# Norms of a fifth chunk off TensorE, Gram sums of batch 0 in other PSUM banks, and a new schedule, in a fused attention and gated-feed-forward kernel

## The chip, the cores and the metric

The kernel runs on one core of one Trainium2 chip. The metric is the device time of one execution in microseconds (us). The kernel before takes 273.9 us (median of three runs, 273.01 to 275.34). Every ratio below comes from runs of both kernels taken in the same rounds on the same chip.

The engines are named as the profile names them: PE is TensorE (PEld its weight loads), DVE is VectorE, ACT is ScalarE, POOL is GpSimd and SP is SyncE. A "q" behind a name means that engine's instruction queue, for instance SPq for a DMA that SyncE issues.

## The reference, cut to what matters

```python
B, N, C = 4, 6336, 256                      # q, k, v: f32
qn = q / (norm(q, axis=1) + 1e-6)           # norms over the N rows
kn = k / (norm(k, axis=1) + 1e-6)
a  = softmax(kn.T @ qn / tau)               # 256 x 256 for each batch
x  = v @ a                                  # B*N rows of 256
H  = maximum(x @ w_h, 0)
T  = sigmoid(x @ w_t + b_t)
out = T * H + (1 - T) * x                   # f32
```

All the attention is over channels, so each batch has two stages. Stage 1 sums k^T q, k^T k and q^T q over 6336 rows. Stage 2 multiplies the rows of v by three 256 x 256 matrices (a, a @ w_h, a @ w_t) and puts the results together. A pair is two blocks of 128 rows, and a chunk is 4 pairs (1024 rows); a batch has 6 chunks and a short rest. Chunks are counted through all batches, from 0 to 23.

## The kernel before

A small planner in the kernel's source puts some thousands of tasks in an order for each engine. Every task has a priority, the buffers that it takes and the buffers that it gives back. The parts that the argument touches follow, with cuts marked.

The numbers that the planner works with:

```python
O_BUFS = 7        # output buffers, 1 MB each, one chunk of 4 pairs of rows
LAG = 5           # a chunk's store is held until this many chunks later have begun
UNTIL = 65        # from this slot (pair number) on, stores are no longer held
AHEAD = 15        # a DMA transpose of v is issued so many slots ahead
BY_DMA = 1        # last batch: chunks of v from this one on are transposed by DMA
APART = 4         # chunks of a batch whose q norms are made off TensorE
V_AHEAD = -2
PRIO = {"tr": (-3.47, -0.36), "ev": (3.23, 2.26), ...}   # cut
```

Stage 1. Each step is 128 rows of q and k; the third matmul gives the q norms, and it is left out for chunks below `APART`, whose squares ACT and POOL make:

```python
def stage1(b, s):
    if s == order_of(b)[0]:
        sg_t[b] = [new(f"sg{c}", [P, 512], f32, f"sg{c}_{b}") for c in range(2)]
    ...
    for c in range(2):
        nc.tensor.matmul(sg[c][:, 0:C], kc, qa, start=first, stop=False)
        nc.tensor.matmul(sg[c][:, C : C + P], kc, kc, start=False, stop=False)
        if not apart(b, s // CH):
            nc.tensor.matmul(sg[c][:, C + P : C + 2 * P], qa[:, cs], qa[:, cs], ...)

def apart(b, j):
    return b > 0 and j < APART
```

The output. `result` is DVE's last instruction for a pair of rows, and the first of a chunk takes a fresh output buffer. SyncE stores the chunk and, when the store has landed, the buffer is free:

```python
def new(tag, shape, dt, name):
    return pool_of.get(tag, work).tile(shape, dt, tag=tag, bufs=nbuf[tag], name=name)

def result(b, i):
    ...
    if o == 0:
        og[(b, j)] = new("o", [P, CH, C], f32, f"o{b}_{j}")
    nc.vector.scalar_tensor_tensor(out=ot, in0=h, scalar=0.0, in1=pp, op0=max, op1=subtract)  # cut
```

So that stores do not take the DMA engines from the loads too early, they are held. A copy of 1 KB out of chunk n sits in SyncE's queue ahead of the store of chunk n - LAG. It cannot be issued before DVE has written the first result of chunk n, and the store behind it waits with it:

```python
def hold(b, j):
    nc.sync.dma_start(out=held_row, in_=og[(b, j)][0:1, 0, :])

def plan_holds():
    for x, b, j in chunk_stores:
        n = b * NJ + j + LAG
        y, g = begun.get(n, (None, 1e9))
        if g > UNTIL:
            x.key = max(x.key, UNTIL + 1.6)
            continue
        x.key = g + 1.6
        plan.add("SP", g + 1.5, 0.1, 0, [y], lambda n=n: hold(n // NJ, n % NJ), size=1024)
```

Of the kernel before, what the change touches and what calls it, by code (L numbers as in the profile page):

```python
# [15 lines left out]
P = 128  # L16
# [3 lines left out]
O_BUFS = 7  # L20
LAG = 5
UNTIL = 65
AHEAD = 15
BY_DMA = 1
MOVE = 150e3
APART = 4
V_AHEAD = -2

PRIO = {
    "tr": (-3.47, -0.36), "ev": (3.23, 2.26), "h": (0.45, 0.69), "bias": (3.3, -0.05),  # L30
    "t": (-0.22, 4.42), "relu": (-3.45, 3.58), "x": (-1.14, 3.11), "gate": (2.73, -4.04),
    "prod": (1.3, -1.18), "res": (4.05, 6.98), "s1": (1.48, 0.05), "sq": (6.77, 9.48),
}
POW = 0.75
HEAD = 6
TAIL = 63
EV = BIAS = ("ACT", "DVE")
ENDS = [17.5, 46, 64.5]

# [13 lines left out]
class Task:  # L53
# [6 lines left out]
    def __init__(self, eng, key, pitch, lat, deps, fn, take=(), drop=(), size=0, follows=()):  # L60
        self.eng, self.key, self.pitch, self.lat = eng, key, pitch, lat
        self.deps, self.fn, self.take, self.drop, self.size = deps, fn, take, drop, size
        self.follows = follows
        self.start = self.done = None
        self.soft = False
        self.held = {}
        self.serial = False
# [11 lines left out]
class Plan:  # L79
# [23 lines left out]
    def run(self):  # L103
# [43 lines left out]
        def pick(e):  # L147
            quiet = e == "POOL" and held(self.sums_stop)
            best = min(
                (x for x in avail[e] if ready(x) and not (quiet and x.soft)),  # L150
                key=lambda x: (x.key, x.n), default=None,
            )
            lst = in_order.get(e)
            if best is None and lst and ready(lst[-1]) and not (e == "POOL" and held(self.loads_stop)):
                return lst[-1]
            return best

        def held(stops):
            return any(
                a.start is not None and (b.done is None or b.done > t + eps) for a, b in stops  # L160
            )

        while left or any(queues.values()):
# [38 lines left out]
            for qq in act:  # L202
                if qq[0][1] < 1.0:
                    x = qq.pop(0)[0]
                    finish(x, t + self.LAG)
                    if x.eng == "POOL":
                        lanes[x.lane] = t + self.LAG
# [5 lines left out]
def kernel(  # L213
# [142 lines left out]
    consts = plan.add("POOL", len(plan.tasks), 0.6, 1.5, [], constants)  # L356
    consts.serial = True
    for j in range(1, NJ - 1):
        plan_load("q", 0, j)
        plan_load("k", 0, j)  # L360
    for nm in "qk":
        plan_load(nm, 0, NJ)
    for part in range(4):
        plan_load("q", 0, NJ - 1, 4, part)
        plan_load("k", 0, NJ - 1, 4, part)
    plan_load("q", 1, 0)
    plan_load("k", 1, 0)
    w_ld = [
# [3 lines left out]
        for m, w in enumerate((moe_w_h, moe_w_t))  # L372
    ]
    b_ld = [
        plan.add("POOL", len(plan.tasks), 0.54, 0, [], lambda u=u: load_b(u), size=40000)
        for u in range(2)
    ]
# [35 lines left out]
    def order_of(b):  # L413
# [4 lines left out]
        return [*range(S - CH), *range(S, NS), *range(S - CH, S)]  # L418

    def stage1(b, s):  # L420



        if s == order_of(b)[0]:
            sg_t[b] = [new(f"sg{c}", [P, 512], f32, f"sg{c}_{b}") for c in range(2)]
        sg = sg_t[b]
# [14 lines left out]
    def apart(b, j):  # L441
        return b > 0 and j < APART

# [25 lines left out]
    def plan_squares(b):  # L469

        ends, x = {}, None
        for j in range(APART):
            key = slot_of((b - 1) * NS + CH * j) + PRIO["sq"][0]
            parts = [
                plan.add(
# [5 lines left out]
            ends[j] = parts  # L481
            n0 = len(plan.tasks)
            y = plan.add(
# [7 lines left out]
            for z in plan.tasks[n0:]:  # L491
                z.soft = True
        def over_partitions():
# [22 lines left out]

    def plan_chain(b, first, last, key, sums_of_q):

# [82 lines left out]

        gs = act(copy_g, 0.58, 0.7, [dk], drop=[(first, "sg0"), (first, "sg1")])
        iq = dve(lambda: (recip(0), dcat()), 0.82, 0.92, [nq, dk])
# [310 lines left out]
    def plan_stage1(b):  # L914
        x = first = None
        part_ends, sums_of_q = ({}, []) if not apart(b, 0) else plan_squares(b)
        for n, s in enumerate(order_of(b)):
            key = -100 + n if b == 0 else slot_of((b - 1) * NS + s) + PRIO["s1"][0]
            deps = loaded("q", b, s) + loaded("k", b, s) + ([x] if x else [])
            x = plan.add(  # L920
                "PE", key, 0.33 if apart(b, s // CH) else 0.44, 0.66, deps, lambda s=s: stage1(b, s),
                take=["sg0", "sg1"] if n == 0 else [],
                drop=([] if apart(b, s // CH) else drops("q", b, s)) + drops("k", b, s),
            )
            x.lat = x.pitch if n < NS - 1 else 0.66
            if apart(b, s // CH) and s % CH == CH - 1:
                plan.add("NONE", 0, 0, 0, [x] + part_ends[s // CH], None, drop=drops("q", b, s))
            first = first or x
        ready[b] = plan_chain(b, first, x, -50, [sums_of_q] if apart(b, 0) else [])
        if b == B - 1:  # L930
            ends_of["sg0"] = ends_of["sg1"] = [x]
# [140 lines left out]
```

## Time and profile before

| | before |
|---|---|
| time, median (runs) | 273.9 us (273.01 to 275.34) |
| span of the profiled run | 271.6 us, clock 0.985 |
| PE's work, by start-to-start times | 239.0 us |
| PE: first matmul, last matmul | 9.0 us, 263.8 us |
| from the last matmul to the end | 7.8 us |
| 1 MB store, issue to landing, median | 9.1 us |

"PE's work" is not the busy time of the page. It adds the distance from each matmul's start to the next where the two follow each other closely, and counts the rest as lost. First start + work + lost = last start: 9.0 + 239.0 + 15.9 = 263.8 us (rounded).

The prediction below shows the page and the stretch around 40 us. What it does not show, and what also belong here, are two rows of the page: DVE's last instruction of a pair (L858) among the costliest groups, with its idle time after the second bar, and the store among the DMA issues.

```profile
L858 DVE SCALAR_TENSOR_TENSOR o<-h,pp 128x512 f32<-128x512 f32 x96 | 65.3, 687 | 1.9
L435 PE MATMUL sg<-q 128*128 128x128 f16 x192 | 42.8, 223 | 0.0
...
out_dram<-o SPq DMA_DIRECT2D x23, 1024.0 KB, 9.1
```

DVE waited only 1.9 us in all ahead of 96 such instructions: output buffers were always free in time. And here is the same kernel by stretch of time (the columns are the stretch, its length, then busy us and instruction count of PE, PEld, DVE, ACT and POOL, the granted clock, the DMA share and the GB/s written):

```profile
110.00:140.00 30.00, 30.00 (x308) 27.58 (x306) 23.09 (x41) 26.58 (x47) 21.00 (x23) 1.00 1.06 267
140.00:170.00 30.00, 29.67 (x301) 26.40 (x299) 24.16 (x61) 25.19 (x48) 16.13 (x19) 1.00 1.06 263
...
200.00:230.00 30.00, 29.48 (x279) 25.32 (x278) 23.47 (x58) 25.27 (x54) 4.09 (x7) 1.00 1.05 306
```

In these stretches PE is full, or nearly so, at full clock.

SyncE's own timeline shows how a held store leaves. Columns are start, length, engine and line; L897 is the 1 KB copy that holds, L872 the store.

```profile
124.93 0.51 SPq L897 DMA_DIRECT2D held_row<-o  x1
125.48 0.58 SPq L872 DMA_DIRECT2D out_dram<-o  x1
```

Chunk 7's first result was written at 124.21 us; the store that it releases was issued 1.27 us later.

### The profile page before, as it was taken

To read this page: it belongs to the slowest core of one execution; us is meant where nothing else is said; L and a number is where in the kernel's file an instruction comes from. 1 tells how busy PE (TensorE), PEld (TensorE's weight loads), DVE (VectorE), ACT (ScalarE), POOL (GpSimd) and SP (SyncE) were. 2 spreads that over 40 slices of the span, in tenths; PEclk is the share of its full clock that TensorE was granted. 3 is DMA by queue.
4 is the path that set the end of the run, shared out by engine and by line. 5 is a ranking of instruction groups with operands and counts; after the bars stand their busy time and mean duration, and the time that the engine had idled before them with its cause. 6 is when DMAs were issued, how large, how long until landed. Compare 5 with 4: busy or idle time off the path is not lost.

```text
span 271.6 us, 6265 instructions
## 1 busy us (share of the span) xinstructions
PE 247.0 (91%) x2447; PEld 218.6 (80%) x2447; DVE 177.8 (65%) x366; ACT 191.5 (71%) x361; POOL 115.3 (42%) x153
## 2 busy tenths in 40 slices
PE   0697859999999999999999999999999999999980
PEld 0596757798999988999999888999998778878870
DVE  1000033658757897778777886767766888999991
ACT  1000034868969888889897888887875989988970
POOL 7221668596691095566928167775002110000000
PEclk9999997999999999999999999999999999999996
DMA  6999999999999999999999999999999999999996
GB/s 109 212 216 214 199 208 214 214 213 215 215 211 215 212 214 219 284 233 279 289 277 255 257 289 233 270 255 275 268 288 272 330 320 316 203 345 279 283 417 241
DMA packets 28430, 68.29 MB, mean 251 GB/s; under 512 B 13168, under 2 KB 15856, under 8 KB 25456
## 3 DMA queue, kind: packets, MB, share of 16 engines
q0 software_dynamic: 13184, 39.20, 73.6%
q1 hardware_dynamic: 15216, 28.69, 30.5%
q8 instruction: 19, 0.31, 0.4%
q14 instruction: 11, 0.09, 0.1%
HBM read 78.38 MB, written 25.95 MB: 384 GB/s over the span
## 4 chain that ended last, share of the span: by engine, by line
PE 76%; DMA 13%; DVE 4%; ACT 2%; issue 2%; POOL 1%; DVEq 0%; ACTq 0%; POOLq 0%
PE d L778 15%; PE h L778 15%; PE t L778 15%; DMA k<-in_k_dram 13%; PE sg L432 12%; PE sg L433 6%; PE vtps L738 6%; PE sg L435 2%; PE ah L667 1%; DVE pp L839 1%; PE t L809 1%; DVE o L858 1%; ACT d L818 1%; ACT uu L832 1%; PE eps L657 1%
## 5 line engine op out<-in xcount | busy, mean ns | idle before, releaser
L778 PEld LDWEIGHTS <-vtsb 128*128 128x128 f16 (+1 forms) x948 | 90.0, 99 | 13.4 <-issue 3.0
L432 PE MATMUL sg<-q,k 128*128 128x256 f16 x384 | 85.7, 278 | 15.2 <-DMA k<-in_k_dram 15.1
L839 DVE SCALAR_TENSOR_TENSOR pp<-uu,d 128x512 f32<-128x512 f32 (+1 forms) x100 | 67.7, 683 | 25.0 <-PE d L778 14.8
L433 PE MATMUL sg<-k 128*128 128x128 f16 x384 | 78.8, 224 | 0.0
L832 ACT ACTIVATE uu<-t 128x512 f32<-128x512 f32 (+1 forms) x100 | 59.5, 599 | 18.6 <-PE t L778 17.2
L858 DVE SCALAR_TENSOR_TENSOR o<-h,pp 128x512 f32<-128x512 f32 x96 | 65.3, 687 | 1.9
L818 ACT ACTIVATE d<-h 128x512 f32<-128x512 f32 (+1 forms) x100 | 57.8, 585 | 5.3 <-PE h L778 4.0
L432 PEld LDWEIGHTS <-k 128*128 128x128 f16 x384 | 38.5, 100 | 18.6 <-DMA k<-in_k_dram 15.9
L450 ACT ACTIVATE sq<-q 128x1024 f32<-128x1024 f16 x24 | 25.0, 1052 | 36.0 <-DMA q<-in_q_dram 36.0
L778 PE MATMUL t<-mr,vtsb 128*128 128x256 f16 x316 | 47.2, 272 | 0.4 <-ACT t L513 0.3
L778 PE MATMUL d<-mr,vtsb 128*128 128x256 f16 x316 | 46.5, 272 | 0.3 <-ACT d L818 0.2
L778 PE MATMUL h<-mr,vtsb 128*128 128x256 f16 x316 | 46.5, 272 | 0.3 <-DVE ri L635 0.3
L435 PE MATMUL sg<-q 128*128 128x128 f16 x192 | 42.8, 223 | 0.0
L433 PEld LDWEIGHTS <-k 128*128 128x128 f16 x384 | 38.3, 100 | 1.5 <-issue 0.3
L456 POOL TENSOR_TENSOR sq<-sq,sq 128x1024 f32<-128x1024 f32 x12 | 28.4, 2368 | 22.3 <-ACT sq L450 22.3
L513 ACT COPY t<-bias_all 128x512 f32<-128x512 f32 (+1 forms) x61 | 36.1, 592 | 1.3
L738 PE MATMUL vtps<-ident,v 128*128 128x128 f32 x144 | 27.9, 275 | 0.5 <-DVE vtsb L515 0.5
L549 DVE SCALAR_TENSOR_TENSOR junk<-sg,ident 128x128 f32<-128x128 f32 x16 | 4.6, 288 | 36.1 <-PE sg L435 35.5
L778 PEld LDWEIGHTS <-vT 128*128 128x128 f16 x240 | 23.4, 98 | 4.5 <-issue 0.5
L311 POOL DMA_DIRECT2D v<-in_v_dram x24 | 13.3, 555 | 31.1 <-PE vtps L738 21.9
L515 DVE COPY vtsb<-vtps 128x256 f32<-128x256 f32 (+2 forms) x42 | 17.6, 419 | 10.0 <-PE vtps L738 9.9
L311 POOL DMA_DIRECT2D q<-in_q_dram x27 | 15.1, 558 | 16.0 <-DMA q<-in_q_dram 8.9
(77 smaller groups left out, 252.1 us busy)
## 6 DMA issues: line engine op xcount, KB each, us to landing
out_dram<-o SPq DMA_DIRECT2D x23, 1024.0 KB, 9.1
v<-in_v_dram POOLq DMA_DIRECT2D x24, 512.0 KB, 18.1
q<-in_q_dram POOLq DMA_DIRECT2D x23, 512.0 KB, 16.7
k<-in_k_dram POOLq DMA_DIRECT2D x23, 512.0 KB, 17.6
out_dram<-o SPq DMA_DIRECT2D x2, 512.0 KB, 6.3
out_dram<-ot SPq DMA_DIRECT2D x4, 192.0 KB, 5.8
q<-in_q_dram POOLq DMA_DIRECT2D x4, 128.0 KB, 8.6
k<-in_k_dram POOLq DMA_DIRECT2D x4, 128.0 KB, 6.6
```

Of the source, the lines that this page charges most:

```text
L311: nc.gpsimd.dma_start(out=t[:, s : s + n, :], in_=main_rows(src)[:, j * CH + s : j * CH + s + n, :])
L432: nc.tensor.matmul(sg[c][:, 0:C], kc, qa, start=first, stop=False)
L433: nc.tensor.matmul(sg[c][:, C : C + P], kc, kc, start=False, stop=False)
L435: nc.tensor.matmul(sg[c][:, C + P : C + 2 * P], qa[:, cs], qa[:, cs], start=False, stop=last)
L456: add(out=sq, in0=sq, in1=other)
L513: nc.scalar.copy(out=out, in_=in_)
L738: nc.tensor.transpose(ps[:, u, 0:nr], v.bitcast(f32), ident0[0:nr, 0:nr])
L778: nc.tensor.matmul(out[0:nr, u, :], vt[u][kt][:, 0:nr], mr[kt][:, col * C : (col + 1) * C], **flags(u, kt))
L818: nc.scalar.activation(out=d[0:nr, :, :], in_=ps_t["h", b, i][0:nr, :, :], func=Act.Relu, scale=0.5)
L832: nc.scalar.activation(out=uu[0:nr, :, :], in_=ps_t.pop(("t", b, i))[0:nr, :, :], func=Act.Tanh, scale=-0.5)
L839: nc.vector.scalar_tensor_tensor(out=pp[0:nr, :, :], in0=el.pop(("uu", b, i))[0:nr, :, :], scalar=1.0, in1=ps_t.pop(("d", b, i))[0:nr, :, ...
L858: nc.vector.scalar_tensor_tensor(out=ot, in0=ps_t.pop(("h", b, i))[0:nr, :, :], scalar=0.0, in1=el.pop(("pp", b, i))[0:nr, :, :], op0=AluO ...
```

## The change

The intent is to take PE work away where PE is full and to shorten the pause of batch 0's softmax. There are four parts:

1. Batch 0's Gram sums go to the two PSUM banks of h, so that batch 1's sums can start at once; the first q and k chunk of batch 1 come in halves, squares of batch 1 wait while the softmax chain runs, and the bias loads go to the front of the load queue.
2. The q norms of five instead of four chunks a batch are made by ACT and POOL.
3. In the last batch, v comes by DMA transpose only from its third chunk on, not from its second.
4. A new order: stores are held for 6 chunks instead of 5 but only to slot 54, transposes go 20 slots ahead, v loads move forward, and all priorities and the ends of the segments are new.

```diff
-LAG = 5
-UNTIL = 65
-AHEAD = 15
-BY_DMA = 1
-MOVE = 150e3
-APART = 4
-V_AHEAD = -2
+LAG = 6
+UNTIL = 54
+AHEAD = 20
+BY_DMA = 2
+MOVE = 165e3
+APART = 5
+V_AHEAD = 0
 ... (PRIO: all values new; TAIL 63 -> 64)
-ENDS = [17.5, 46, 64.5]
+ENDS = [17.5, 44.5, 67.5]
 ... (the planner learns to hold back squares of one batch)
     consts = plan.add("POOL", ..., constants)
+    b_ld = [plan.add("POOL", ..., lambda u=u: load_b(u), size=4000) for u in range(2)]
     for j in range(1, NJ - 1):
         plan_load("q", 0, j)
         plan_load("k", 0, j)
 ...
-    plan_load("q", 1, 0)
-    plan_load("k", 1, 0)
+    for part in range(2):
+        plan_load("q", 1, 0, 2, part)
+        plan_load("k", 1, 0, 2, part)
 ...
-    b_ld = [plan.add("POOL", ..., lambda u=u: load_b(u), size=40000) for u in range(2)]
     plan_load("v", 0, 0)
 ...
+    def sg_tag(b, c):
+        return f"sg{c}" if b else "h"
 ...
-            sg_t[b] = [new(f"sg{c}", [P, 512], f32, f"sg{c}_{b}") for c in range(2)]
+            sg_t[b] = [new(sg_tag(b, c), [P, 512], f32, f"sg{c}_{b}") for c in range(2)]
```

`O_BUFS` stays at 7. The diff does not touch it.

## The prediction

> **What bounds the kernel now.** I read the page first, then the busy time by stretch, the chain of waits, and last the timeline around the one place where PE stands still. From the page:
>
> ```profile
> span 271.6 us, 6265 instructions
> ...
> PE 247.0 (91%) x2447; PEld 218.6 (80%) x2447; DVE 177.8 (65%) x366; ACT 191.5 (71%) x361; POOL 115.3 (42%) x153
> ...
> PEclk9999997999999999999999999999999999999996
> DMA  6999999999999999999999999999999999999996
> ...
> PE 76%; DMA 13%; DVE 4%; ACT 2%; issue 2%; POOL 1%; DVEq 0%; ACTq 0%; POOLq 0%
> ```
>
> PE makes up 76% of the chain that ended last, DMA 13%, and there is one slice (41 to 47 us) with a reduced PE clock. The DMA engines are busy in every slice too, so there may be two bounds. The busy time by stretch (us of stretch, then PE, PEld, DVE, ACT, POOL busy, clock, DMA share, GB/s written):
>
> ```profile
> 32.00:40.00 8.00, 5.51 (x75) 5.06 (x73) 2.21 (x14) 1.94 (x3) 5.97 (x11) 1.00 1.15 207
> 40.00:44.00 4.00, 3.47 (x19) 2.22 (x20) 1.93 (x9) 1.69 (x7) 2.69 (x6) 0.69 1.16 215
> 44.00:48.00 4.00, 3.68 (x30) 2.75 (x28) 0.81 (x3) 2.64 (x5) 3.35 (x3) 0.88 1.07 214
> ...
> 52.00:56.00 4.00, 4.00 (x45) 3.67 (x44) 3.01 (x6) 3.65 (x6) 2.36 (x2) 1.00 1.07 214
> ...
> 240.00:260.00 20.00, 20.00 (x177) 17.07 (x176) 18.64 (x29) 17.96 (x35) 0.00 (x0) 1.00 1.06 297
> ```
>
> Up to 37 us batch 0 is loaded and PE follows the loads. From 52 us PE is full. Between lies the softmax chain of batch 0. Busy is a modelled figure, so I took the start-to-start times of the matmuls instead: 109 ns for 256 columns, 55 ns for 128. By them PE has 239.0 us of work; it starts at 9.0, its last matmul starts at 263.8, and after 37.3 us it loses 9.8 us: 3.2 in one gap, 1.7 at half clock, 4.9 scattered over 220 us. The gap, in the timeline:
>
> ```profile
> 37.29 0.22 PE L435 MATMUL sg<-q 128*128 128x128 f16 x1
> ...
> 38.06 2.00 ACT L450 ACTIVATE sq<-q 128x1024 f32<-128x1024 f16 x2 [36.04 <-DMA q<-in_q_dram]
> ...
> 39.97 0.63 ACT L600 COPY gs<-sg 128x256 f32<-128x256 f32 x2
> ...
> 40.53 0.28 PE L432 MATMUL sg<-q,k 128*128 128x256 f16 x1 [3.02 <-DMA k<-in_k_dram]
> ```
>
> and the chain of waits through it (start, us, what):
>
> ```profile
> 31.99 8.49 DMA k<-in_k_dram
> ...
> 41.04 0.48 PE cqb L608 x2
> ...
> 42.70 0.43 PE bias_t L880
> 43.12 0.85 PE bias_d L880 x2
> ```
>
> Three things delay the chain. PE's program order puts the first Gram matmul of batch 1 ahead of cqb, and it waits for k of batch 1, landing at 40.48. ACT spends 2.00 us on squares of batch 1 before it copies the Gram sums out. And the three bias matmuls stand in PE's order in the middle of it, at half clock. V of batch 0 had landed at 44.35; its first transpose started at 47.30 and the first h at 48.91.
>
> DMA: loads write 213 GB/s of f16, so they read 426 GB/s of f32, and they land without a pause until 207 us. Comparing landings with first uses, v has 1.4 to 5 us of margin over most of batches 0 to 2 (least 1.39 us, batch 1, sixth chunk), q and k 1.7 to 4.7 us up to 80 us and 8 to 19 us later. So PE can't run far ahead without starving.
>
> **What the Trainium skill says.** "TensorE: Matmul & The Clock Gate", Part 1 (the HAM clock gate): activity is judged in free-running windows of 3413 ns, and after an idle one the clock is halved. This trace agrees: its clock record is 0.5 from 41.45 to 44.86 us, 3.41 us, right after a window in which PE worked only from 40.53. It also gives 55.6 ns for warm 128-column matmuls; the trace has 55. "Perfetto Trace Analysis", Identifying the Most-Contended Engine, warns that matmul busy share misleads, hence the start-to-start times. "DMA: Bandwidth & Descriptors", Specifications, names 435 GB/s as the ceiling of the 16 engines; the 426 measured agrees, so load order matters and more requests cannot help. "PSUM — Partial Sum Buffer", summary of rules, asks to guard by bank and to evacuate promptly: all eight banks are assigned here, so batch 1's Gram sums must wait for the copy out of sg until batch 0 has other banks. No run yet shows what that wait costs alone, since k lands at about the same time.
>
> **The change part by part.**
>
> *Start of batch 1.* Batch 0's sums go to the two h banks, idle until the fold, so sg is free for batch 1 at once. The first q and k chunks of batch 1 come in halves: the last batch-0 part landed at 35.58, and a chunk takes 2.45 us, so both first halves should be there at 38.0 instead of 40.5. Half a chunk is 4 steps of 0.33 us (two of 0.109 and two of 0.055 each) = 1.3 us of PE work moved into the gap. Squares of batch 1 are held back during the chain, so the copy can start at about 38.75, not 39.97. The bias loads go to the front of the queue and their three matmuls (0.65 us warm, 1.28 as run) into the load phase. Then cqb can run at about 39.85 when dcat is done (39.76), rather than 41.04, eps near 42, the folds by 43.5, mr at about 44.2. Now v, landing at 44.35, is the last to come: transposes at once, first h at about 45.3 to 45.8, against 48.91. This is a gain of about 2.9 us in PE's stream. Part is given back: from there PE has 6.1 us of work for the first v chunk (4 pairs of 1.53), then waits on q,k at 49.3 (2.6 us of work) and 54.3; ACT and DVE also need 3.55 us a pair together, 1.78 each. I charge 0.8 us. Net **2.1 us**.
>
> *Norms of a fifth chunk.* 3 batches x 8 steps x 2 matmuls x 0.0545 = **2.6 us** off PE, all in the stretch where PE is full. It adds 3 x 2 squares of 1.05 us = 6.3 us on ACT and 3 x (2.37 + 1.29 + 1.47) = 15.4 us on POOL, 42% busy. ACT and DVE are together at 83% from 80 to 160 us, so this mostly fits; it costs some scattered waits.
>
> *A second chunk of the last v through PE.* 16 transposes x 0.056 = **0.9 us** added to PE, plus four evacuations of 0.42 (DVE) or 0.59 (ACT) us. One of five full DMA transposes goes. By the packets' times the transposes hold the 16 engines for about 16 us after 207 us, so one is worth about 3 us of DMA time, and 4.9 us of SP's issue time, which now blocks stores behind it.
>
> *Order.* v loads two slots earlier relative to q and k, stores held one chunk longer but only to slot 54, transposes 20 slots ahead, new priorities. These don't remove work; they decide whether the DMA queue can feed a faster PE. In the last 12 us stores are queued up (418 GB/s from 260 to 265), and from the last matmul to the end there are 7.7 us. Fewer and earlier transposes should leave this less crowded: **0.6 us**, a guess between 0 and 2.
>
> Sum: 2.1 + 2.6 - 0.9 + 0.6 = 4.4 us; 273.9 - 4.4 = 269.5. I put the centre a little lower, at 269.3, for the clock below.
>
> **The rivals.**
> 1. *DMA takes the bound.* For it: loads land back to back until 207 us, v's margin is below 3 us at many chunks, and a PE 4 us ahead would use them up. Against: q and k of batches 2 and 3 arrive 8 to 19 us early, v moves forward at their cost, and 3 us of DMA work goes. If it wins, PE waits for v appear in batches 0 to 2 and the gain shrinks to 1 to 2 us: 272 to 273.
> 2. *The clock.* With half a chunk worked at 38 us, the window may count as active and the 1.7 us at half clock go (some of them in time where PE starves anyway): then 268 to 268.5. Or pauses at 39.4 to 40.5 and 42 to 45 us halve it later, when PE is full: 271.
> 3. *ACT and DVE take the bound.* 6.3 us of squares plus about 2 of evacuations. After slot 67 the DVE was already 18.64 of 20 us busy. If this wins, PE's scattered loss rises from 4.9 to 7 us: 271.5.
> 4. *The gain at the start is hidden anyway*, since v lands at 44.35 in both; then only the work removed counts: 271.5.
>
> **Range and chances.** All parts well: 266.5. Rival 1 or 3: 272 to 273. The runs before span 2.3 us by themselves. Eight in ten: 266.6 to 272.2. Faster by 2% needs 268.4, a little beyond my centre: 0.34. Slower by 2% would need a stall of 10 us: 0.03.
>
> **What would show it.** Right, if the first sg matmul of batch 1 starts near 38.1 us and the first h before 46; if the L435 group falls from 192 to 144 matmuls; if PE's last matmul starts near 259.5; if the half-clock record is gone or moved. The steps fail if PE waits for v or k longer than 1 us after 46 us; if DVE's or ACT's waits on each other grow in the last 60 us; or if the time from the last matmul to the end exceeds 8 us because the stores come out late.

## The result

The changed kernel took **286.36 us** (median of 4 runs, 283.24 to 287.03) against 274.33 us of the kernel before in the same rounds (4 runs). The ratio is 1.042, with a 95% interval of 1.033 to 1.051: slower, outside the predicted range on the far side. A ratio is computed as the mean time of one kernel's fast runs over that of the other's of the same rounds, so it is not quite the ratio of the medians quoted. All profiles compared here are of fast runs unless it is said.

The page of the changed kernel, the lines that answer to those shown of before:

```profile
span 285.3 us, 6194 instructions
...
PE 250.1 (88%) x2415; PEld 217.6 (76%) x2415; DVE 181.2 (64%) x375; ACT 194.9 (68%) x362; POOL 131.7 (46%) x167
...
PEclk9999999999999999999997999999979999999996
DMA  6999999999999999999999899999999999999994
...
PE 47%; DMA 37%; DVE 5%; ACT 4%; issue 3%; SPq 1%; POOL 1%; DVEq 0%; ACTq 0%; POOLq 0%
DMA out_dram<-o 24%; DMA k<-in_k_dram 13%; PE t L790 10%; PE h L790 10%; PE d L790 9%; PE sg L444 7%; PE sg L445 4%; PE vtps L750 3%; DVE o L870 2%; ACT uu L844 1%; PE sg L447 1%; PE t L821 1%; DVE pp L851 1%; SPq L909 1%; ACT d L830 1%
...
L870 DVE SCALAR_TENSOR_TENSOR o<-h,pp 128x512 f32<-128x512 f32 x96 | 65.6, 686 | 13.1 <-DMA out_dram<-o 9.1
...
L447 PE MATMUL sg<-q 128*128 128x128 f16 x144 | 32.5, 226 | 0.0
...
out_dram<-o SPq DMA_DIRECT2D x23, 1024.0 KB, 10.4
```

PE's share of the chain that ended last fell from 76% to 47%. What came in is stores: `out_dram<-o` is 24% of the chain, and it had no place among the first fifteen before. DVE's last instruction of a pair (L870, which was L858) now waits 13.1 us in all, 9.1 of them for a store. The clock row has two new dips, in the slices at 150 and 208 us, and the one at 41 us is gone. The q-norm group fell from 192 to 144 matmuls, as the change meant it to.

The list of waits (what waited, for what: us in total, times, longest) shows the wait and how it reaches PE:

```profile
DVE o L870 <- DMA out_dram<-o: 9.1, 6, 2.4
PE h L790 <- DVE o L870: 8.9, 7, 2.0
...
DVE o L870 <- issue: 2.5, 1, 2.5
```

DVE waited for a store six times, and a seventh time (2.5 us, at 206.9 us) where the profile names no releaser but where a store had landed 0.08 us earlier. PE waited for DVE seven times, because h's bank is given back by that same DVE instruction.

By stretch, PE is no longer full:

```profile
110.00:140.00 30.00, 27.66 (x282) 25.16 (x281) 20.57 (x37) 23.48 (x41) 21.89 (x25) 1.00 1.06 246
140.00:170.00 30.00, 27.18 (x251) 23.48 (x250) 21.87 (x56) 23.39 (x45) 14.07 (x17) 0.94 1.00 241
...
200.00:230.00 30.00, 27.44 (x245) 23.27 (x243) 21.14 (x53) 24.67 (x50) 8.59 (x10) 0.94 1.07 328
```

By start-to-start times PE has 237.3 us of work instead of 239.0, but loses 30.7 us between its first and last matmul instead of 15.9. Of the added 14.8 us, 13.0 lie between 110 and 230 us (15.2 against 2.2). Here is the first of these waits in the timeline of the changed kernel (start, length, engine; the idle time ahead and what ended it stand in brackets):

```profile
125.17 0.60 PE L790 MATMUL d<-mr,vtsb 128*128 128x256 f16 x4
...
126.11 0.69 DVE L870 SCALAR_TENSOR_TENSOR o<-h,pp 128x512 f32<-128x512 f32 x1 [1.76 <-DMA out_dram<-o]
...
126.83 0.51 SPq L909 DMA_DIRECT2D held_row<-o  x1
126.85 0.60 PE L790 MATMUL h<-mr,vtsb 128*128 128x256 f16 x4 [1.08 <-DVE o L870]
...
127.38 0.63 SPq L884 DMA_DIRECT2D out_dram<-o  x1
```

and the chain of waits through it (start, us, what):

```profile
115.68 10.33 DMA out_dram<-o
...
126.11 0.70 DVE o L870
...
126.83 0.51 SPq L909
...
127.38 9.95 DMA out_dram<-o
```

Read together, these are a closed loop. The store of chunk 0 was issued at 115.68 and landed at 126.01. Only then can chunk 7, which needs chunk 0's buffer, be begun (126.11). The start of chunk 7 releases the store of chunk 1, issued 1.27 us later (127.38), landing at 137.33; chunk 8 begins at 137.42, chunk 9 at 149.04. One turn is 1.27 + 10.0 = 11.3 us, while a chunk takes some 9.2 us in the kernel before (chunks 7, 8, 9, 10 began 9.18, 9.32, 9.31 and 8.78 us after the one ahead of them). The same table for both kernels, first write of a chunk minus landing of the store that frees its buffer, in us:

| chunk | 7 | 8 | 9 | 10 | 11 | 12 | 13 | 14 |
|---|---|---|---|---|---|---|---|---|
| before | 10.32 | 6.48 | 8.82 | 6.68 | 10.40 | 12.87 | 9.68 | 5.93 |
| changed | 0.09 | 0.09 | 0.09 | 0.02 | 1.56 | 0.09 | 0.12 | 0.08 |

In the changed kernel seven of these eight chunks begin at the instant their buffer comes free. From chunk 15 on the margin is 6 us and more, since the stores are no longer held from slot 54.

The two new dips of the clock follow the longest of these pauses. PE stood still for 2.18 us at 147.5 and for 2.12 us at 205.5; the clock record is half from 150.55 to 153.96 us and from 208.58 to 211.99 us, 3.41 us each, at a cost of some 1.7 us each (an estimate: half of 3.41). The distance between them is 58.03 us, which is 17.0 times 3.413.

The start moved the way that was predicted, but less far: the first Gram matmul of batch 1 began at 38.93 us (40.53 before; predicted near 38.1), the first h at 46.72 (48.91 before; predicted before 46). Later the two kernels can't be compared pair by pair, as their orders differ: the changed kernel was 2.2 us ahead at the pair counted 28 (117.48 against 119.71) and 1.5 us behind at the pair counted 32 (129.04 against 127.50), but the same kernel with one more buffer, which does not wait there, also goes from 1.0 us ahead to 1.5 us behind.

**The buffer theory.** The time comes from output buffers: with LAG 6 and seven buffers, chunk n needs the buffer of chunk n - 7, whose store is released only when chunk n - 1 begins, so a store has one chunk's time to land and needs longer. **The rival, a slower DMA:** the waits for stores are a symptom, because DMA as a whole is slower in the new order (a store takes 10.4 us instead of 9.1), and with more buffers PE would wait for something else. **For the smaller question**, what became of the predicted gain, the first theory was: apart from the buffers the parts of the change are worth what the prediction says, so with buffers the kernel beats the one before by some 2 us or more.

### The profile page after: what moved, and what is told of

The parts are those of the page before. It is cut to its first block, busy times and chain, and to the rows that moved or that the text cites. A ratio compares the mean times of both kernels' runs of the same rounds, so it can differ in the third digit from the quotient of the medians.

```text
span 285.3 us, 6194 instructions
## 1 busy us (share of the span) xinstructions
PE 250.1 (88%) x2415; PEld 217.6 (76%) x2415; DVE 181.2 (64%) x375; ACT 194.9 (68%) x362; POOL 131.7 (46%) x167
## 4 chain that ended last, share of the span: by engine, by line
PE 47%; DMA 37%; DVE 5%; ACT 4%; issue 3%; SPq 1%; POOL 1%; DVEq 0%; ACTq 0%; POOLq 0%
DMA out_dram<-o 24%; DMA k<-in_k_dram 13%; PE t L790 10%; PE h L790 10%; PE d L790 9%; PE sg L444 7%; PE sg L445 4%; PE vtps L750 3%; DVE o L870 2%; ACT uu L844 1%; PE sg L447 1%; PE t L821 1%; DVE pp L851 1%; SPq L909 1%; ACT d L830 1%
## 5 line engine op out<-in xcount | busy, mean ns | idle before, releaser
L790 PEld LDWEIGHTS <-vtsb 128*128 128x128 f16 (+1 forms) x996 | 96.2, 100 | 26.6 <-issue 13.7
L444 PE MATMUL sg<-q,k 128*128 128x256 f16 x384 | 82.5, 277 | 13.7 <-DMA k<-in_k_dram 13.6
L870 DVE SCALAR_TENSOR_TENSOR o<-h,pp 128x512 f32<-128x512 f32 x96 | 65.6, 686 | 13.1 <-DMA out_dram<-o 9.1
L830 ACT ACTIVATE d<-h 128x512 f32<-128x512 f32 (+1 forms) x100 | 58.2, 584 | 10.7 <-PE h L790 9.8
L790 PE MATMUL h<-mr,vtsb 128*128 128x256 f16 (+1 forms) x332 | 50.0, 275 | 8.9 <-DVE o L870 8.9
L790 PE MATMUL t<-mr,vtsb 128*128 128x256 f16 (+1 forms) x332 | 50.7, 276 | 1.8 <-ACT t L525 1.4
L444 PEld LDWEIGHTS <-k 128*128 128x128 f16 x384 | 38.0, 99 | 17.9 <-DMA k<-in_k_dram 15.3
L790 PE MATMUL d<-mr,vtsb 128*128 128x256 f16 (+1 forms) x332 | 50.7, 276 | 0.5 <-ACT d L830 0.5
L468 POOL TENSOR_TENSOR sq<-sq,sq 128x1024 f32<-128x1024 f32 x15 | 35.4, 2358 | 33.8 <-ACT sq L462 33.8
L445 PEld LDWEIGHTS <-k 128*128 128x128 f16 x384 | 38.1, 99 | 1.2
L447 PE MATMUL sg<-q 128*128 128x128 f16 x144 | 32.5, 226 | 0.0
L462 ACT ACTIVATE sq<-q 128x1024 f32<-128x1024 f16 x30 | 31.2, 1052 | 0.0
L527 DVE COPY vtsb<-vtps 128x256 f32<-128x256 f32 (+1 forms) x48 | 20.1, 419 | 9.7 <-PE vtps L750 9.5
L316 POOL DMA_DIRECT2D v<-in_v_dram x24 | 13.5, 561 | 26.7 <-DMA vT<-v 21.5
L790 PEld LDWEIGHTS <-vT 128*128 128x128 f16 x192 | 18.7, 98 | 3.5 <-issue 0.2
L316 POOL DMA_DIRECT2D q<-in_q_dram x28 | 15.6, 556 | 10.6 <-DMA q<-in_q_dram 6.4
## 6 DMA issues: line engine op xcount, KB each, us to landing
out_dram<-o SPq DMA_DIRECT2D x23, 1024.0 KB, 10.4
q<-in_q_dram POOLq DMA_DIRECT2D x22, 512.0 KB, 15.3
```

What stands on the lines that cost most here:

```text
L462: nc.scalar.activation(out=sq, in_=qa, func=Act.Square)
L468: add(out=sq, in0=sq, in1=other)
L790: nc.tensor.matmul(out[0:nr, u, :], vt[u][kt][:, 0:nr], mr[kt][:, col * C : (col + 1) * C], **flags(u, kt))
L830: nc.scalar.activation(out=d[0:nr, :, :], in_=ps_t["h", b, i][0:nr, :, :], func=Act.Relu, scale=0.5)
L870: nc.vector.scalar_tensor_tensor(out=ot, in0=ps_t.pop(("h", b, i))[0:nr, :, :], scalar=0.0, in1=el.pop(("pp", b, i))[0:nr, :, :], op0=AluO ...
```

## The experiments

Sixteen kernels ran. All gave correct results except one that stores only half the output on purpose. Medians are in us; "before" is the kernel before in the same rounds. The expectations are quoted as they were put on record before each run, with the letters that their theories had at that time (A is the buffer theory); the text after each says in words what stood and what fell.

### The buffers: two one-line changes, and one of LAG

**One more output buffer in the changed kernel.** Only the allocation changes; the planner still counts seven, so the order of instructions on every engine is identical to that of the changed kernel (compared engine by engine).

```diff
-  tile(shape, dt, tag=tag, bufs=nbuf[tag], name=name)
+  tile(shape, dt, tag=tag, bufs=nbuf[tag] + (tag == "o"), name=name)
```

> The changed kernel, its instruction order on every engine the same, with an eighth output buffer allocated. Theory A (a store held until the sixth next chunk has begun leaves the seven buffers no slack, so VectorE waits for the store's landing and PE behind it): the seven waits of 0.02 to 0.12 us after a landing (chunks 7 to 10 and 12 to 14) go, the idle time of VectorE before o that a landing of a store ends falls from 9.1 us to under 0.5, the two half-clock records at 150 and 208 us go, and the time falls from 286.4 to 271 to 273 us (the 14 us of additional PE loss go, 3 us less PE work remains). Rival B (the order of loads, the earlier flush of stores at slot 54 and a saturated DMA are what costs): at most 2 us are gained, 284 or more. Rival C (ScalarE and GpSimd with the fifth chunk of squares): also 284 or more.

Measured: 275.61 (274.62 to 277.95, 11 runs) against 274.30; ratio 1.0053 (1.0025 to 1.008). That is 10.8 us less than the changed kernel, with the same instructions in the same order. In the list of waits no wait of DVE for a store is left. By stretch, PE is full again:

```profile
110.00:140.00 30.00, 30.00 (x308) 27.67 (x307) 22.09 (x40) 25.35 (x44) 23.19 (x27) 1.00 1.06 245
140.00:170.00 30.00, 29.17 (x289) 25.77 (x288) 23.68 (x59) 26.11 (x52) 18.01 (x22) 1.00 1.06 264
```

The stores still take 9.3 to 10.7 us at these chunks, and chunks 7 to 10 and 12 to 14 now begin 0.4 to 3.0 us *before* the landing that they would have had to wait for with seven buffers. PE's loss from 110 to 230 us falls from 15.2 to 3.3 us, the half-clock records at 150 and 208 us are gone, and the last matmul is 12.0 us earlier. So the waits were the cause, and the rival falls: a store takes as long as in the changed kernel, and yet no wait of that size took the place of these. The size expected, 271 to 273, was missed by some 3 us, which the next section takes up.

**One output buffer less in the kernel before**, again in the allocation alone and with the same order of instructions. If the rule is (buffers - LAG) chunks of time for a store to land, then 6 and 5 must fail as 7 and 6 do.

```diff
-  tile(shape, dt, tag=tag, bufs=nbuf[tag], name=name)
+  tile(shape, dt, tag=tag, bufs=nbuf[tag] - (tag == "o"), name=name)
```

> The kernel before, its instruction order the same on every engine, with six output buffers in place of seven: the store of a chunk is then issued only one chunk before its buffer is needed, as in the changed kernel. Theory A: VectorE waits at the first write of chunks 6 or 7 to 14 or so, 1 to 2.5 us each, and the time rises from 274.3 to 283 to 288 us. Rivals B and C: nothing else changed, so 274 to 276.

Measured: 286.92 (285.62 to 289.49, 4 runs); ratio 1.0486 (1.041 to 1.056). The kernel before, with none of the change in it, loses 12.6 us in the same way. Its list of waits:

```profile
DVE o L858 <- DMA out_dram<-o: 8.1, 4, 3.4
...
PE h L778 <- DVE o L858: 6.6, 4, 2.7
```

Chunk 7 begins at 129.88 us, right after chunk 1's store landed at 129.79; chunk 10 at 162.34, after 162.25; chunk 12 at 186.10, after 185.97. A half-clock record at 142.96 us follows here too. Some 2.3 us of the delay in this profile stood already at the first h (51.20 us), where the clock was half for 6.83 us instead of 3.41; that part isn't due to buffers. The other three runs had a higher mean clock (0.977 to 0.983 against 0.973) and took 285.62 to 289.49 us, so the loss does not rest on it.

**LAG 5 in the changed kernel**, with its seven buffers. This gives a store two chunks' time again, but the planner then makes another order.

```diff
-LAG = 6
+LAG = 5
```

> The changed kernel with LAG 5 in place of 6 and all else kept; the planner makes another order of it. Theory A: the first writes of chunks have 5 us or more after the landing of the store that frees their buffer, and the time is 268 to 273 us. Rival B: above 280, as the order of loads and the flush at slot 54 stay.

Measured: 279.89 (279.33 to 280.33, 4 runs); ratio 1.0204. The output margins are 6 us and more and no wait for a store is left, so 6.5 us came back. But it missed its 268 to 273. PE now loses 5.6 us between 200 and 230 us. By what the profile names as having ended each of these losses, 4.0 us are waits for ACT, 1.0 for the rest of k and 0.5 for DVE. The loads come later too: at seven of the twelve chunks of batches 1 and 2 v lands only 0.04 to 0.9 us ahead of its first transpose, and from 46 us on PE waits 1.7 us in all for v. Whether LAG 6 was meant to clear the way for the loads is a guess. The experiment can't tell, since more than one thing moves in the order.

### Where the predicted 4.4 us went

**The start part alone, on the kernel before** (parts of 1: other banks, halves, held squares, bias loads first; all numbers of the planner as before).

```diff
+    b_ld = [plan.add("POOL", ..., lambda u=u: load_b(u), size=4000) for u in range(2)]   # ahead of the second q load
-    plan_load("q", 1, 0); plan_load("k", 1, 0)
+    for part in range(2): plan_load("q", 1, 0, 2, part); plan_load("k", 1, 0, 2, part)
-    sg_t[b] = [new(f"sg{c}", ...)]
+    sg_t[b] = [new(sg_tag(b, c), ...)]                                                   # "h" for batch 0
 ... (the rest of part 1 of the change)
```

> The kernel before with the start of the change alone: Gram sums of batch 0 in the banks of h, halves for the first chunk of batch 1, bias loads first, squares held during the chain; all parameters and the chunk counts as before. By the prediction's step this is worth 2.1 us: 271.5 to 273. If the gain at the start is hidden later (v and the DMA queue bound the middle), 274 to 275.

Measured: 275.21 (274.03 to 276.53, 12 runs); ratio 1.0031 (1.0007 to 1.0056). The first h came 1.6 us earlier (47.30), but at pair 12 it was 0.4 us ahead, at pair 24 0.2 us, and from pair 36 to 72 within 0.13 us of the kernel before. The predicted 2.1 us were not kept. One reason stands at the very start of POOL's timeline, where the second load of q (L316) waits behind the bias loads (L294), and these wait for a memset on DVE:

```profile
1.24 0.67 POOL L316 DMA_DIRECT2D q<-in_q_dram  x1 [0.79 <-POOLq L1066]
...
4.32 1.00 POOL L294 DMA_DIRECT2D btb<-in_moe_b_t_dram  x2 [1.29 <-DVE half L286]
5.32 0.55 POOL L316 DMA_DIRECT2D q<-in_q_dram  x1
```

In the kernel before the second load of q was issued at 2.97 us:

```profile
2.97 0.56 POOL L311 DMA_DIRECT2D q<-in_q_dram  x1
```

POOL issues in order, so two small loads in the wrong place put off the issue of the third load by 2.3 us, and those behind it with it. Batch 0's last Gram matmul starts at 38.28 us instead of 37.29.

**The bias loads after the third chunk instead**, once in the changed kernel with eight output buffers and once in the start part alone.

```diff
-    b_ld = [plan.add("POOL", ..., lambda u=u: load_b(u), size=4000) for u in range(2)]
+    b_ld = []
     for j in range(1, NJ - 1):
         plan_load("q", 0, j)
         plan_load("k", 0, j)
+        if j == 2:
+            b_ld += [plan.add("POOL", ..., lambda u=u: load_b(u), size=4000) for u in range(2)]
```

> The changed kernel with the eighth output buffer, and its two bias loads moved from the second place of the load queue to behind the third chunk. In the run with eight buffers GpSimd waited 1.28 us for VectorE's memset of the bias tile and spent 1.00 us on the two issues, so the second q load was issued at 5.3 us, not 3.0, and every batch-0 chunk landed 0.8 to 2 us later than in the kernel before. Theory D (the whole first 207 us are bound by the load queue, so a late start of it is carried to the end): the second q load is issued near 3.0 us, stage 1 of batch 0 ends near 37.2 us in place of 38.4, and the time falls by 0.8 to 1.5 us to 274.1 to 274.8. Rival E (PE is the bound after 45 us and the start is made up later): within 0.4 us of 275.6.

> The kernel before with the start of the change alone, bias loads behind the third chunk. It has the whole gain that the prediction put at 2.1 us and no late loads. Theory D: the first h comes at about 46.3 us, 2.6 us earlier than before, but by the sixth v chunk (about 90 us) PE is within 0.5 us of the kernel before, because v and k then start to be used within 0.3 us of their landing; time 273.7 to 274.5. Rival E: the gain stays to the end, 271.8 to 273.

Measured: 273.97 (273.44 to 275.06, 22 runs; ratio 0.9992, 0.9976 to 1.0008) and 274.06 (272.79 to 277.06, 22 runs; ratio 0.9997, 0.9976 to 1.0018), against 274.24. The changed kernel with eight buffers gains 1.6 us from this alone (275.61 to 273.97; the two were run in different calls, with the kernel before at 274.30 and 274.24), so that delay was carried to the end. But both now merely equal the kernel before.

In the first, PE's work is 237.2 us, 1.7 less than before, which is what the prediction reckoned (2.6 less, 0.9 more), and its last matmul starts at 263.83 us, as before. What is saved is lost again: PE loses 17.5 us instead of 15.9. From 37.3 to 52 us it loses 5.0 instead of 5.9, so the start did gain; but from 52 to 110 us 2.9 instead of 1.0, and from 200 us on 2.9 instead of 2.0. In batch 0 each chunk of v now lands 0.04 to 1.0 us ahead of its first transpose, where it was 2.0 to 3.5 us in the kernel before. Yet of the loss from 52 to 110 us only 0.4 us are waits for v and 0.4 for k, by what ended them; 1.5 us are waits for ACT (0.5 before). From 46 us to the end PE loses 7.6 us instead of 5.0, and 5.1 of them end with ACT instead of 2.9. The tail is 8.7 us instead of 7.8.

In the second, the first h is 2.2 us ahead; at pair 8 0.8 us are left, from pair 36 to 72 0.5 us. Its first four chunks of v land 0.14 to 0.24 us ahead of use. What PE waits for in batch 0, though, is k of batch 1: 0.65 us at 49.6 and 0.58 at 61.7, each ended by a landing of k (50.26, 62.31). So here loads do take back most of what the start had gained.

**The fifth chunk alone**, on the start part with late bias loads, at LAG 5 and seven buffers (on the kernel before itself the planner finds no order with it).

```diff
-APART = 4
+APART = 5
```

> The same with the q norms of a fifth chunk off TensorE, at LAG 5 and seven buffers. The prediction's step: 2.6 us less of PE work, all of it gained, so 2.6 us under the run without it. Theory D: the loads can't come earlier with the same stores between them, so v lands just before its use in batches 1 and 2 (margins under 0.5 us) and less than 1 us is gained.

Measured: 278.33 (276.61 to 280.82, 6 runs); ratio 1.0133. PE's work fell by 2.8 us, to 236.4, as reckoned. The loss rose by more: from 46 us on from 7.5 us to 15.3. v lands 0.04 to 0.15 us ahead of use at five chunks of batches 1 and 2, which looks like the cause, but the list of waits says otherwise. First without the fifth chunk, then with it (PE alone, from 46 us on; what waited, for what: us in total, times, longest):

```profile
PE d L792 <- ACT d L832: 0.4, 1, 0.4
PE t L792 <- ACT t L527: 0.3, 1, 0.3
```

```profile
PE t L792 <- ACT t L527: 2.4, 5, 0.6
PE d L792 <- ACT d L832: 2.3, 3, 1.5
...
PE vtps L752 <- DMA v<-in_v_dram: 0.5, 1, 0.5
```

By start-to-start times 9.0 of the 15.3 us end with ACT (3.0 of 7.5 without the fifth chunk), 2.2 with DVE and 3.8 with loads and transposes. ACT is the engine that makes the added squares. The planner's order differs, so this shows that work taken from PE is not a gain by itself here; it does not show what the fifth chunk costs.

**The fourth chunk again, in the good version** (changed kernel, eight buffers, late bias loads; the segment ends had to go back as well).

```diff
-APART = 5
+APART = 4
-ENDS = [17.5, 44.5, 67.5]
+ENDS = [17.5, 46, 64.5]
```

> The same base (eight buffers, late bias loads) with four chunks of q norms and with the stage-1 ends 46 and 64.5 of the kernel before, as the planner finds no order for four chunks with the new ends. The prediction's step says that the fifth chunk is worth 2.6 us of PE work: 276 to 277 without it. If its gain is taken back by waits for ScalarE, GpSimd and loads, as the run with five chunks at LAG 5 suggests: 273.5 to 274.8.

Measured: 276.17 (274.92 to 281.5, 14 runs); ratio 1.0061. By the ratios of fast runs (two of the 14 were slow) that is 1.9 us more than the good version, with some 3 us more PE work. With output buffers enough, the fifth chunk is worth a good part of the 2.6 us predicted, though the ends were changed with it.

### The last 60 us

**Half of each chunk stored**, on the changed kernel with eight buffers. The result is wrong on purpose; it measures what the stores cost.

```diff
-    out=main_rows(ob)[:, j * CH + s : j * CH + s + n, :], in_=og[(b, j)][:, s : s + n, :]
+    out=main_rows(ob)[:, j * CH + s : j * CH + s + n // 2, :], in_=og[(b, j)][:, s : s + n // 2, :]
```

> The changed kernel with eight buffers, storing only half of each chunk (a wrong result on purpose; order on all engines but the sizes of stores the same). It takes 12 MB, about 29 us at 420 GB/s, from the DMA engines after 115 us. Theory D: the v chunks of batches 1 and 2 land several us before use (in the run with whole stores the margins were 0.1 to 3 us), PE's loss after 110 us falls, and the queue of stores at the end goes: 4 to 7 us faster, 269 to 271.5. Rival E: PE needs what it needs; only the last 8.7 us shrink, by 1 to 2.5 us: 273 to 274.5.

Measured: 272.37 (271.66 to 274.29, 12 runs); ratio 0.9936. PE's losses by stretch from 110 to 260 us are the same to 0.1 us, although from chunk 11 to 17 v now lands 4.8 to 18.2 us early instead of 0.1 to 3.1. So with eight buffers it is not the loads of v that set PE's pace after 110 us. By what ended them, 3.0 of the 3.4 us lost there are waits for ACT; no run takes work off ACT alone to test it. What moved is the tail, from 8.7 to 6.1 us: stores cost some 2.6 us at the end.

**UNTIL 65, BY_DMA 1 and BY_DMA 3**, each on the good version, to see whether the tail or the last batch can be bettered by one number.

```diff
-UNTIL = 54        # first kernel
+UNTIL = 65
-BY_DMA = 2        # second kernel: 1, third kernel: 3
+BY_DMA = 1
```

> The changed kernel with eight buffers and late bias loads (274.0 us), stores held to slot 65 as before the change, not 54. In that run eight stores are issued together at 188 us and 3 v loads of the last batch wait behind them; its DMA transposes start at 222 us only, and 7 stores are left at 253 us, so 8.7 us pass from the last matmul to the end, against 7.8 before. Theory F (the early flush pushes the transposes, and they the stores, into the last 40 us): the first transpose is issued before 215 us, the last stretch falls to under 8 us, and the time to 272.5 to 273.5. Against it: fewer stores are out by 222 us, so more are left at the end, 9 us or more and 274.5 to 276.

> The same base with v of the last batch by DMA from its second chunk on, as before the change: 16 transposes (0.9 us) less on PE and one DMA transpose more. The prediction's steps: PE's last matmul 0.9 us earlier (263 us), the stretch after it 0.6 to 2 us longer; 273.5 to 275.5 in sum.

> The same base with v of the last batch by DMA only from its fourth chunk. PE gets another 0.9 us, the DMA engines lose another transpose, about 3 us. If the crowded end matters most, the stretch after the last matmul falls from 8.7 to about 7 and the time to 273 to 273.8; if PE and the evacuations do (VectorE is busy 9.4 of 10 us after 235 us), 274.5 to 276.

Measured: UNTIL 65 gave 277.15 (275.95 to 278.44, 6 runs; ratio 1.0093) with a tail of 9.9 us, so the theory that the change's earlier end of the hold is what lengthens the tail found no support (the planner's order moves with it). BY_DMA 1 gave a median of 280.10 over all 6 runs (276.52 to 280.87; ratio of the fast ones 1.016); its profile fell in a slow run, so I take only that PE's work fell by the 0.9 us that the prediction had for these 16 transposes, to 236.3. BY_DMA 3 gave 276.73 (276.34 to 277.03, 6 runs; ratio 1.0081): its tail is 5.9 us, but its last matmul is at 269.2 us. Of the three values the change's own is the fastest with its priorities; they were not set anew for the others.

**Stores from another queue.** SyncE issues the last transposes and the stores in one order, so a store waits behind a transpose. Here the last eight chunks' stores are issued by GpSimd, once on the good version and once on the kernel before.

```diff
+    eng = nc.gpsimd if b * NJ + j >= 16 else nc.sync
-    nc.sync.dma_start(out=main_rows(ob)..., in_=og[(b, j)]...)
+    eng.dma_start(out=main_rows(ob)..., in_=og[(b, j)]...)
```

> The changed kernel with eight buffers and late bias loads (274.0 us), the stores of the last eight chunks and the last tail issued from GpSimd's queue instead of SyncE's, where they stand behind DMA transposes of some 5 us each. In the run without it chunk 17 was complete at about 230 us and its store issued at 245, three stores left at 253, and 8.7 us pass from the last matmul to the end. Theory G (PE's saving is there, but stores blocked on SyncE pile up and take 2 to 3 us of it at the end): each of these stores is issued within 2 us of its chunk's last result, the stretch after the last matmul falls to 5.5 to 6.5 us, and the time to 271.3 to 272.2. Rival H (the DMA engines themselves are full, whoever issues): the stretch stays over 8 us, 273.5 to 275.

> The kernel before with the same change of queue alone. Theory G: its last stretch of 7.8 us falls to about 6, and the time by 1.5 to 2 us to 272.2 to 272.8. Rival H: 274 to 275.

Measured: 299.06 (292.64 to 300.37) and 295.37 (288.37 to 296.98), 6 runs each; the runs spread so far that all but the fastest count as slow, and no ratio is given. The reason is in the list of waits of the first:

```profile
POOL v L316 <- DMA vT<-v: 20.0, 1, 20.0
...
PE t L792 <- DMA vT<-v: 17.1, 1, 17.1
```

A transpose issued at 240.5 us landed at 267.8, and PE stood still for 17 us. On the kernel before the same edit brings the same wait, 17.2 us, one time. In the first, from 240 to 252 us the packets of GpSimd's queue take 98% of the 16 engines' time and those of SyncE's, where the transpose stands, 11% (the two overlap); from 252 to 266 us it is 36% and 79%. What was expected fell: SyncE's one order does not cost time here. It seems to keep the stores out of the way of the transposes. Both profiles are of slow runs, but the wait of 17 us is in both.

**Seven buffers for v**, in the allocation alone, on both kernels. In the changed kernel and in the good version POOL waits some 20 us for a transpose to give back a buffer of v, and the last loads of v come late for it.

```diff
-  bufs=nbuf[tag] + (tag == "o")
+  bufs=nbuf[tag] + (tag == "o") + 2 * (tag == "v")     # on the kernel before: bufs=nbuf[tag] + 2 * (tag == "v")
```

> The changed kernel with eight output buffers and late bias loads (274.0 us), seven v buffers allocated in place of five, the order on every engine the same. There GpSimd waits 20.5 us, to 229 us, for a DMA transpose to land before it may load the next to last v chunk into its buffer; the later transposes stand in SyncE's order ahead of stores. Theory G2 (the late transposes keep stores back to the end): that wait goes, the third and fourth transposes are issued by 240 us, fewer stores are left after 253 us, the stretch after the last matmul falls from 8.7 to 6.5 to 8 us, and the time to 272 to 273.5. Rival H: v was in time anyway, and the loads only take the DMA engines from the stores of 188 to 228 us; within 0.5 us of 274.0.

> The kernel before with seven v buffers, the order the same. GpSimd's waits for v buffers (38 us in four waits of 4 to 16 us) shrink, so v lands earlier from 190 us on, but its margins there were 9 to 18 us. Theory G2: the transposes come some us earlier and the stores at the end too, 272.5 to 273.7. Rival H: 274 to 274.8.

Measured: 275.11 (274.09 to 276.19; ratio 1.0024, 1.0006 to 1.0042) and 275.40 (272.98 to 279.61; ratio 1.0016, 0.9994 to 1.0038), 22 runs each, against 274.45. In the good version POOL's wait is gone and the last loads of v are issued at 208 to 210 us instead of 229, yet the transposes land at 236.7, 241, 248 and 253 us and the tail is 9.3 us (9.1 on the kernel before). The loads now stand beside transposes and stores, which all share the DMA engines. To take away the wait that the profile showed on POOL gained nothing.

No version with a correct result beat the kernel before by more than the noise; the best, the changed kernel with eight output buffers and late bias loads, equals it (273.97 against 274.24).

## Why the prediction was wrong, point by point

1. **The step that failed is "Order".** It said of the stores held one chunk longer that they "don't remove work; they decide whether the DMA queue can feed a faster PE", and entered 0.6 us of gain. A store that is held keeps its buffer, and the step never counted the seven output buffers. It was worth 10.8 us of loss, measured by one buffer more with nothing else changed, and again 12.6 us in the kernel before with one buffer less (of the profiled run's loss, some 2.3 us stood before any buffer was short). None of the four rivals was this wait, and "slower by 2% would need a stall of 10 us: 0.03" dismissed just such a stall.
   The profile of before had all that was needed. A chunk takes 9.2 us; a held store leaves 1.27 us after its chunk begins and takes 9.1 us in the median to land, up to 10.9 us among the held ones. Needed: 10.4 us or more. Given with 7 buffers and LAG 5: two chunks, 18.4 us. With LAG 6: one chunk, 9.2 us. The shortfall is 1.2 us or more for six of the eight chunks from 7 to 14 (chunks 11 and 12, at the batch's end, take 11 to 12 us even before), so some 7 us at the least, and more with the 9.7 us that the stores of chunks 0 to 7 took on the mean. It was there to be reckoned blind.
2. **The half clock.** Rival 2's first half was right: the record at 41 us went. Its fear that pauses halve the clock later was right in kind, but not where it looked for them: two records came at 150 and 208 us, behind pauses of 2.1 to 2.2 us for output buffers, and their 3.4 us are part of the loss in point 1.
3. **Start of batch 1.** The mechanism was right, but of its three signs only the vanished record came as stated: the first sum matmul began at 38.9 us, not near 38.1, and the first h at 46.7, not before 46. The size was off: 2.1 us were entered, and from pair 36 on nothing was left in the start part alone, 0.5 us with the bias loads mended. Three terms were mis-sized. Moving the bias loads was taken as free and cost 1.6 us in the changed kernel. In the start part with that mended cqb ran at 39.96 us (39.85 expected), but v landed at 44.79, not 44.35, and the last part of mr came off DVE at 45.63, not near 44.2, so the first h was 2.2 us ahead and not 3.1 or more (2.9 were entered for PE's stream). And the 0.8 us given back were 1.7 (2.2 us ahead at the first h, 0.5 at pair 36); 1.2 us of it are the two waits for k, which the prediction had named. The sign set for rival 1, a wait of PE for v or k of over 1 us after 46 us, did not come in the changed kernel: the longest is 0.6.
4. **Norms of a fifth chunk** (2.6 us) and **a second chunk of the last v through PE** (0.9 us). As changes of PE's work both were right: 239.0 to 237.2 us, and singly 2.8 and 0.9. As changes of the time, the first is worth about 1.9 us where buffers suffice; at LAG 5 it is eaten by new waits, 6 of the added 7.8 us of them for ACT.
5. **The end.** The guess that fewer and earlier transposes leave the end less crowded failed: the tail is 8.3 us, 8.7 with eight buffers, against 7.8 (one profile each; over 8 us was the sign that the prediction had set for its failing). Stores are 2.6 us of it. What bounds the last 40 us otherwise stays open: more v buffers and a longer hold did not help, and another queue for the stores hurt. I have shown what it is not.
6. **ACT and DVE** (rival 3). In the changed kernel this was hidden behind the buffers. POOL's busy time rose by 16.4 us, where 15.4 were reckoned, and ACT's by 3.4. But with the buffers and the bias loads set right, what rival 3 had said came: PE's scattered loss was to rise from 4.9 to 7 us, and from 46 us on it is 7.6 instead of 5.0, with 5.1 ended by ACT instead of 2.9. This is read from what the profile names as the end of each wait; no run lightens ACT alone.
7. **Two readings** of the profile are off without weight: the half-clock record stands at 41.51 to 44.92 us, and the 426 GB/s is worked out (twice the 213 GB/s that the trace shows written), not measured; the ceiling set beside it is the page's for the ports into SBUF.

So of the predicted 4.4 us, with the buffers and the bias loads set right, nothing remains: in the profiled runs 1.7 us of work are gone from PE, its losses grew by 1.6 us (less at the start, 2.6 us more from 46 us on), and the tail grew by 1.0 us (span 272.6 us against 271.6, while the medians of the two are equal).

## What to carry to other kernels

Whenever a change holds a buffer longer, by a later store or a deeper prefetch, count the buffers: those not held, times the pace of the loop, must cover the time from the release of the transfer to its landing, and take the landing time from a trace of the loaded machine. Test it with one buffer more or less in the allocation alone, since the order of instructions then stays the same and the difference is the wait and what follows from it. And a gain in one engine's work is a gain in time only as far as the loads and the other engines keep up. A small margin of a load is not yet a wait: list what ends each of the engine's waits before adding up the work.

## What the Trainium skill lacked or had wrong

- "DMA: Bandwidth & Descriptors", Bandwidth, measured table: 6.15 us for 1 MB, for a load issued by GpSimd with the other core of the pair idle. The 1 MB stores of these kernels, issued by SyncE beside loads, landed after 9.1 us (before) and 10.4 us (changed) in the median. The page has no time from issue to landing for a store beside loads, and that is the one which sets how many buffers are needed. The same page gives 261 GB/s for a DMA transpose (Latency and other measured facts), which would be an estimate of 2.0 us for 512 KB; here transposes took 6.3 to 26.2 us from issue to landing in the changed kernel, and up to 27.4 and 39.0 us in the two kernels with stores of another queue.
- "Perfetto Trace Analysis", Identifying Performance Opportunities, says that the same gap repeating on an engine that should be full can mean too few buffers. This case agrees (gaps of 1.2 to 2.2 us on PE once in 11.3 us), but the page gives no way to reckon it ahead from hold, landing time and pace.
- "TensorE: Matmul & The Clock Gate", HAM oscillation, puts its rule as no idle gaps above about 3.4 us. Here gaps of 2.18 and 2.12 us were followed by 3.41 us at half clock, while gaps of 1.24 to 1.64 us were not. A longer one, 2.65 us by the busy times (127.97 to 130.63 us in the kernel before with six buffers), was not followed either. The page's free-running window fits this: in each of the 18 traces the changes of the clock record lie whole multiples of 3.413 us apart (the two records above 17.0). Cut on that grid, from the first full clock to the last matmul, the traces have 1,326 windows at full clock. PE was idle for 1.95 to 3.41 us in the ten that a half-clock record follows, and for at most 1.90 us in the others; the edge at 129.31 us splits the gap of 2.65 us into 1.3 and 1.3. So here idle time within one window counted, and under 2 us of it was enough. PE's ends are modelled, and no run moved a gap on purpose.
- No page that I read reckons what a load that has to wait costs the loads behind it in GpSimd's queue: here two bias loads that waited 1.29 us for a memset put them 2.3 us later.
